# A fused attention and MLP block on one core: load order at the start, denominator, a norm's transposes and two chunks' output sums

## The chip, the cores and the metric

The kernel runs on one core of one Trainium2 chip. The core has five engines that work side by side, each in its own fixed order: TensorE (PE in the profile, with PEld for its weight loads), VectorE (DVE), ScalarE (ACT), GpSimd (POOL) and SyncE (SP). DMA transfers are issued from the queues of SP, ACT and POOL and run beside them. The metric is the device time of one execution in microseconds (us); lower is better.

## The reference

The input `x` has 2048 rows of 512 in bf16. One layer norm, attention in 32 heads of 16 in which each position sees 8 positions (itself and those 2, 4, ... 14 before it), an output projection and a residual; then a second norm, a gated MLP of width 1376 and a second residual.

```python
def _layernorm(x, axis=-1, eps=1e-5):
    m = jnp.mean(x, axis=axis, keepdims=True)
    v = jnp.var(x, axis=axis, keepdims=True)
    return (x - m) / jnp.sqrt(v + eps)
...
        H = 32; Dh = D // H
        W, dil = 8, 2
        qkv = (lambda x, *d: x.transpose(*d))((x @ wqkv).reshape(B, S, 3, H, Dh), 2, 0, 3, 1, 4)
        q, k, v = qkv[0], qkv[1], qkv[2]
        scale = Dh ** -0.5
...
        logits = jnp.einsum("bhsd,bhswd->bhsw", q, kg) * scale
        logits = jnp.where(mask[None, None, :, :], logits, -1e9)
        attn = _softmax(logits, axis=-1)
        o = jnp.einsum("bhsw,bhswd->bhsd", attn, vg)
        return (lambda x, *d: x.transpose(*d))(o, 0, 2, 1, 3).reshape(B, S, D) @ wo
...
        gate = jnp.einsum("bsd,df->bsf", x, W_gate)
        up = jnp.einsum("bsd,df->bsf", x, W_up)
        gate = gate * (lambda x, dt: x.astype(dt))(gate > 0, gate.dtype)
        h = gate * up
        return jnp.einsum("bsf,fd->bsd", h, W_down)
...
    h = x + _A_ref(_layernorm(x, axis=-1), A_wqkv, A_wo)
    h2 = h + _B_ref(_layernorm(h, axis=-1), B_W_gate, B_W_up, B_W_down)
```

## The kernel before

The 2048 rows are four chunks (`tk` 0 to 3) of 512 rows, each of four tiles of 128 rows. `x` stays in SBUF as `x_sm`, and the first residual is added into it in place. All weights are loaded once and stay.

Each chunk goes through these steps. First norm (`layernorm` without `residual`): VectorE takes statistics of each tile (L454, L457), ScalarE makes the reciprocal deviation with Ln and Exp (L467, L471), VectorE normalises (L489), TensorE transposes by four 128x128 matmuls a tile (L518), and ScalarE copies the result out of PSUM (L534; in chunk 0 VectorE does so for tiles 1 and 3, L532). Projections: 12 blocks of four matmuls each (L559), 512 columns wide, which ScalarE copies out (L567) to `qT`, `kT`, `vT`. Logits: VectorE forms products of q with shifted k (L608; in halves in chunk 0, L623), TensorE sums them within each head by a selection matrix (L614), ScalarE takes Exp (L672), which leaves two tiles `ex` of 512 columns, each with four of the eight positions. Denominator: two matmuls into one bank, one for each `ex` (L692), then Ln and Exp on ScalarE (L695, L698). In chunks 1 to 3 VectorE multiplies the `ex` tiles by the reciprocal (L716), and SP broadcasts them over partitions by DMA (L732); in chunk 0 TensorE does the broadcast (L743). VectorE multiplies with shifted v (L764; L779 in chunk 0) and adds up the eight positions: the first of three adds is in chunks 0 to 2 an accumulating DMA of 512 KB issued on POOL (L807), the others run on VectorE (L767, L801 or L771). Output projection: 16 matmuls (L833), residual and row sums (L842 on ScalarE in chunk 0, L844 on VectorE after). Second norm: as the first, with squares on ScalarE (L443); five tile pairs of the second norms are transposed by DMA from SP (`DMAT`, L507) and not by TensorE. MLP: per 128 of the width one block of four matmuls for up and one for gate (L906), copied out by ScalarE (L910 to one of two `up_sb` tiles, L913), multiplied by VectorE (L934); the last 96 of the width go another way (L873 to L892). Down projection: 11 matmuls for each of the four row tiles (L952); VectorE adds the residual from `x_sm` (L963), SP stores 128 KB (L969).

What each engine does in which order is not the source's order. `plan.add` records every step with an engine, a duration, what it waits for and which buffers it takes; `Plan.order` lays the steps out in time by these assumed durations, and of two steps of one engine the one with the lower number in the hand-kept list `RANK` goes first. Buffers come from small pools: 8 PSUM banks, five `row` tiles, two `up_sb` tiles, five `big` tiles. So every engine has one fixed order, and a step that waits holds up everything behind it on its engine. The DMA queues of SP and POOL are such orders too.

At the start `setup` issues the loads. SP takes x tiles 0 and 2, then q and k weight slabs 0 and 2, then chunk 1's x; ACT takes x tiles 1 and 3 and slabs 1 and 3. The v weights and chunks 2 and 3 are held back by small copies on POOL, which write one element of the destination and so make the load wait. TensorE runs 44 matmuls on an empty tile meanwhile (`NWARM`, L408) and 8 each (`NFILL`, L416) after the first transposes of tiles 0 and 1. `GUIDE` holds the second tile's statistics back behind the first's sums, and the third's behind the second's norm. The first four q and k blocks of chunk 0 are cut in three: both column halves for weight slabs 0 and 1, then all columns for slabs 2 and 3.

Of the kernel before, what the change touches and what calls it, by code (L numbers as in the profile page):

```python
# [55 lines left out]
]  # L56


class Op:

# [31 lines left out]
class Plan:  # L92
# [9 lines left out]
    def add(self, key, *a, **k):  # L102
# [8 lines left out]
        return op  # L111


    GUIDE = (("xag0", 0, "xst1", 0), ("xxn1", 0, "xst2", 0))

    def order(self):
        for kx, cx, ky, cy in self.GUIDE:
            xs = [o for o in self.ops if o.key and o.key[0].startswith(kx) and o.key[1] == cx]
            for o in self.ops:
                if o.key and o.key[0].startswith(ky) and o.key[1] == cy:  # L120
                    o.deps = o.deps + xs
# [900 lines left out]
```

## Time and profile before

| what | value |
|---|---|
| time, median of 3 runs | 198.13 us (197.99 to 198.37) |
| span of the profiled execution, first to last instruction | 196.6 us |
| TensorE busy | 190.5 us, 97% of the span |
| VectorE busy | 154.0 us, 78% |
| ScalarE busy | 111.7 us, 57% |
| GpSimd busy | 12.7 us, 6% |

The profiled execution is known by its span alone; what lies around the span is the rest to the measured time. In the windows, each engine has its busy time and, in brackets, its instructions, then the granted TensorE clock as a share, the mean busy share of the 16 DMA engines, and the GB/s they moved. In the timeline, a row is a run of like instructions: start, time to the last one's end, engine, line, operation, output and inputs, count, and in square brackets the idle time before it with what ended it. In the grouped rows come the count, the busy time and the mean of one in ns, then the idle time before the group. Chunks overlap: TensorE does chunk 2's and 3's projections between 36 and 64 us while chunk 0 is still in its attention.

### The profile page before, as it was taken

The page shows a single profiled execution, that of the slowest core. Times are in us where ns is not written, and L with a number is a line of the kernel's source. Part 1 is how long each engine was busy: PE and PEld are TensorE (multiplying, and loading weights), DVE is VectorE, ACT ScalarE, POOL GpSimd, SP SyncE. Part 2 cuts the span into 40 slices and gives each one's busy share as a digit, 9 for nine tenths or more (in the row PEclk, how much of TensorE's full clock was granted, in tenths as well). Part 3 has the DMA queues.
Part 4 walks back from the last instruction along what each step waited for, and adds up shares of the span by engine and source line. Part 5 has one row for each costly group of instructions (what it writes and reads, how often), then busy time and mean ns, then how long its engine had stood idle before and what let it go on. Part 6 is the DMA issues. An engine that isn't in the chain of part 4 may idle for free.

```text
span 196.6 us, 3034 instructions
## 1 busy us (share of the span) xinstructions
PE 190.5 (97%) x1111; PEld 97.1 (49%) x1131; DVE 154.0 (78%) x251; ACT 111.7 (57%) x234; POOL 12.7 (6%) x28
## 2 busy tenths in 40 slices
PE   7899999999999999999999999999999999999994
PEld 7756445654445434464444435444444655444542
DVE  6779999999999999999999779999686331223233
ACT  3548699984598947694334658505674615235400
POOL 4000000330000013100033000000000000000000
PEclk9999999999999999999999999999999999999999
DMA  6969980695000809947369971411002220030114
GB/s 154 310 202 389 405 262 2 122 198 108 3 0 6 196 15 173 188 89 169 81 130 198 181 204 64 82 29 24 3 0 53 53 57 0 0 107 0 27 57 133
DMA packets 21134, 21.99 MB, mean 112 GB/s; under 512 B 8736, under 2 KB 17920, under 8 KB 21120
## 3 DMA queue, kind: packets, MB, share of 16 engines
q1 hardware_dynamic: 18672, 14.65, 25.9%
q0 software_dynamic: 1728, 6.29, 17.2%
q10 hardware_dynamic: 720, 0.85, 1.4%
q8 instruction: 9, 0.15, 0.3%
q14 instruction: 5, 0.04, 0.1%
HBM read 8.42 MB, written 2.10 MB: 53 GB/s over the span
## 4 chain that ended last, share of the span: by engine, by line
PE 66%; DMA 14%; issue 13%; DVE 4%; POOL 1%; SPq 1%; POOLq 0%; DVEq 0%
PE bank L906 20%; PE bank L559 19%; PE bank L952 14%; DMA big<-big 7%; PE bank L833 5%; DMA wv_sb<-in_A_wqkv_dram 4%; PE bank L614 2%; DVE big L764 2%; PE bank L873 2%; PE bank L518 2%; DMA x_sm<-in_A_x_dram 1%; POOL big L807 1%; DMA big<-ex 1%; DVE big L608 1%; PE bank L836 1%
## 5 line engine op out<-in xcount | busy, mean ns | idle before, releaser
L906 PE MATMUL bank<-quad,wgu_sb 128*128 128x512 bf16 x313 | 72.0, 379 | 0.4
L906 PEld LDWEIGHTS <-wgu_sb 128*128 128x128 bf16 x320 | 31.0, 98 | 37.3 <-issue 0.8
L952 PE MATMUL bank<-wd_sb,gT 128*128 128x512 bf16 (+2 forms) x182 | 40.1, 366 | 0.3
L913 ACT ACTIVATE gr<-bank 128x512 bf16<-128x512 f32 x40 | 23.2, 603 | 26.0 <-PE bank L906 24.5
L910 ACT CAST up_sb<-bank 128x512 bf16<-128x512 f32 x40 | 23.2, 594 | 16.5 <-PE bank L906 14.0
L934 DVE TENSOR_TENSOR gT<-gr,up_sb 128x1024 bf16<-128x1024 bf16 x20 | 13.7, 689 | 22.7 <-ACT up_sb L910 16.8
L559 PE MATMUL bank<-quad,wqk_sb 128*128 128x512 bf16 (+1 forms) x132 | 30.2, 367 | 0.2
L952 PEld LDWEIGHTS <-gT 128*128 128x128 bf16 (+1 forms) x187 | 18.1, 98 | 19.5 <-issue 0.4
L764 DVE TENSOR_TENSOR big<-big,vT 128x4096 bf16<-128x4096 bf16 x12 | 27.0, 2283 | 0.1
L608 DVE TENSOR_TENSOR big<-quad,kT 128x4096 bf16<-128x4096 bf16 x12 | 27.0, 2284 | 0.0
L559 PEld LDWEIGHTS <-wqk_sb 128*128 128x128 bf16 x136 | 14.7, 114 | 13.0 <-issue 2.1
L963 DVE TENSOR_TENSOR row<-x_sm,bank 128x512 bf16<-128x512 bf16 (+1 forms) x17 | 10.8, 651 | 9.2 <-PE bank L952 9.2
L767 DVE TENSOR_TENSOR big<-big 128x1024 bf16<-128x1024 bf16 (+2 forms) x24 | 16.8, 729 | 1.2 <-DMA big<-big 1.2
L559 PE MATMUL bank<-quad,wv_sb 128*128 128x512 bf16 x62 | 15.7, 380 | 0.4 <-DMA wv_sb<-in_A_wqkv_dram 0.3
L807 POOL DMA_DIRECT2D big<-big x12 | 10.5, 874 | 85.0 <-DVE big L764 55.0
L833 PE MATMUL bank<-wo_sb,quad 128*128 128x512 bf16 x62 | 14.7, 379 | 0.4 <-DVE quad L801 0.3
L489 DVE TENSOR_SCALAR row<-x_sm,mv,rs 128x512 bf16<-128x512 bf16 x32 | 11.4, 407 | 1.8 <-ACT rs L471 1.8
L534 ACT COPY quad<-bank 128x1024 bf16<-128x1024 bf16 (+1 forms) x11 | 10.0, 944 | 4.5 <-PE bank L518 4.4
L567 ACT CAST kT<-bank 128x512 bf16<-128x512 f32 x16 | 8.9, 598 | 5.7 <-PE bank L559 5.5
L454 DVE BATCH_NORM_STATS2 st<-x_sm 128x6 f32<-128x512 bf16 x16 | 10.3, 675 | 2.1 <-DMA x_sm<-in_A_x_dram 2.1
L567 ACT CAST quad<-bank 128x512 bf16<-128x512 f32 x16 | 9.5, 607 | 3.6 <-PE bank L559 3.6
L443 ACT ACTIVATE row<-x_sm,mv 128x512 bf16<-128x512 bf16 x12 | 8.6, 714 | 4.2 <-DVE mv L435 4.0
(72 smaller groups left out, 157.5 us busy)
## 6 DMA issues: line engine op xcount, KB each, us to landing
big<-big POOLq DMA_DIRECT2D x12, 512.0 KB, 5.4
big<-ex SPq DMA_DIRECT2D x24, 128.0 KB, 2.7
out_dram<-row SPq DMA_DIRECT2D x15, 128.0 KB, 1.8
x_sm<-in_A_x_dram SPq DMA_DIRECT2D x3, 512.0 KB, 4.9
wgu_sb<-in_B_W_up_dram SPq DMA_DIRECT2D x1, 1376.0 KB, 8.8
wgu_sb<-in_B_W_gate_dram SPq DMA_DIRECT2D x1, 1376.0 KB, 11.8
wd_sb<-in_B_W_down_dram SPq DMA_DIRECT2D x1, 1280.0 KB, 15.2
wqk_sb<-in_A_wqkv_dram SPq DMA_DIRECT2D x2, 256.0 KB, 6.9
```

Source lines behind the costliest of these rows:

```text
L559: nc.tensor.matmul(mm.t[:, lo:hi], lhsT=wv_sb[:, dt, t:D:NT] if c == 2 else wqk_sb[:, dt, c * D + t:(c + 1) * D:NT], rhs=xnT.t[:, dt, lo:h ...
L567: nc.scalar.copy(out=o, in_=mm.t[:])
L608: V.tensor_tensor(out=pb.t[:].rearrange("p (t w) s -> p t w s", t=2), in0=q4, in1=k4, op=ALU.mult)
L764: V.tensor_tensor(out=mt.t[:], in0=ab.t[:], in1=v8, op=ALU.mult)
L767: V.tensor_tensor(out=mt.t[:, 0:n, :], in0=mt.t[:, 0:n, :], in1=mt.t[:, n:2 * n, :], op=ALU.add)
L807: nc.gpsimd.dma_start(mt.t[:, 0:4, :], mt.t[:, 4:8, :], accum_op=ALU.add)
L833: nc.tensor.matmul(od.t[:], lhsT=OT.t[:, t, j * P:(j + 1) * P], rhs=wo_sb[:, t, :], start=(t == 0), stop=(t == NT - 1 and tk not in RPE))
L906: nc.tensor.matmul(mm.t[:fs, lo:hi], lhsT=wgu_sb[:, dt, g, ft * P: ft * P + fs], rhs=hnT.t[:, dt, lo:hi], start=(dt == 0), stop=(dt == NT ...
L910: nc.scalar.copy(out=ub.t[:fs, i, :], in_=um.t[:fs, :])
L913: nc.scalar.activation(out=gr.t[:fs, i, :], in_=gm.t[:fs, :], func=ACT.Relu)
L934: V.tensor_tensor(out=gt.t[:fs, 0:n, :], in0=gr.t[:fs, 0:n, :], in1=ub.t[:fs, 0:n, :], op=ALU.mult)
L952: nc.tensor.matmul(od.t[:, c0:c1], lhsT=gts[ft].t[:fs, ft % 2, j * P:(j + 1) * P], rhs=wd_sb[:fs, ft, c0:c1], start=(ft == 0), stop=(ft == ...
```

## The change

It has five parts and a new `RANK` list of 746 entries in place of 737, which sets a new order on every engine.

1. Start. On each of the two queues x tiles and q, k weight slabs alternate: SP x0, slab 0, x2, slab 2; ACT x1, slab 1, x3, slab 3. Chunk 1's x becomes four loads, held back by a POOL copy until x3 has landed; the v weights are held back until weight slab 3 has landed. The gate, up and down weights are loaded in halves (`f_load`), gate first. `GUIDE` goes; the warm-up is 56 matmuls, the fills are 13 and 10; of chunk 0's tiles only tile 1 is copied out by VectorE. Six q and k blocks of chunk 0 are cut, now by column halves: left half for slabs 0 and 1, left half for 2 and 3, right half for all.
2. Denominator of chunks 1 to 3 (`DEN1`): VectorE adds the two `ex` tiles (into one of the five `row` tiles) and TensorE does one matmul.
3. First norm of chunk 3: normalised on ScalarE (`LNA`), transposed by four DMA transposes on SP (two `x` entries in `DMAT`), which in the order stand behind the last weight load and ahead of chunk 1's broadcasts.
4. Output of chunks 0 and 1 (`ODA`): ScalarE copies two row tiles from PSUM into an `up_sb` tile, a DMA on POOL adds these 256 KB into `x_sm`, and SP stores 256 KB from there.
5. The planner's assumed load times.

`LATE` is empty, so what depends on it does nothing.

```diff
-    GUIDE = (("xag0", 0, "xst1", 0), ("xxn1", 0, "xst2", 0))
...
-    DEN1 = ()
+    DEN1 = (1, 2, 3)
...
+    ODA = (0, 1)
+    LATE = ""
...
-    xn_s = o_s = slots(5, [P, D], BF16, "row")
+    es_s = xn_s = o_s = slots(5, [P, D], BF16, "row")
...
+    def f_load(n, i):
+        if n == "d":
+            lo, hi = (0, 5) if i == 0 else (5, NFF)
+            nc.sync.dma_start(
+                wd_sb[:, lo:hi, :], B_W_down[lo * P:hi * P, :].rearrange("(ft p) n -> p ft n", p=P))
+            if FTAIL and i:
+                nc.sync.dma_start(wd_sb[:FTAIL, NFF, :], B_W_down[NFF * P:F, :])
+        else:
+            w = (B_W_gate if n == "g" else B_W_up).rearrange("(dt p) f -> p dt f", p=P)
+            nc.sync.dma_start(wgu_sb[:, 2 * i:2 * i + 2, int(n == "u"), :], w[:, 2 * i:2 * i + 2, :])
...
-        for j in range(BPC):
-            (nc.scalar if j % 2 else nc.sync).dma_start(x_sm[:, j:j + 1, :], x_rows[:, j:j + 1, :])
-        for dt in range(NT):
-            (nc.scalar if dt % 2 else nc.sync).dma_start(wqk_sb[:, dt:dt + 1, :], w3_r[:, dt:dt + 1, 0:2 * D])
-        nc.sync.dma_start(x_sm[:, BPC:2 * BPC, :], x_rows[:, BPC:2 * BPC, :])
+        for i in range(2):
+            for n, q in enumerate((nc.sync, nc.scalar)):
+                j = 2 * i + n
+                q.dma_start(x_sm[:, j:j + 1, :], x_rows[:, j:j + 1, :])
+                q.dma_start(wqk_sb[:, j:j + 1, :], w3_r[:, j:j + 1, 0:2 * D])
...
-        nc.gpsimd.tensor_copy(out=wv_sb[0:1, 0, 0:1], in_=x_sm[0:1, 0, 0:1])
+        nc.gpsimd.tensor_copy(out=x_sm[0:1, BPC:2 * BPC, 0:1], in_=x_sm[0:1, 3, 0:BPC])
+        for j in range(BPC, 2 * BPC):
+            nc.sync.dma_start(x_sm[:, j:j + 1, :], x_rows[:, j:j + 1, :])
+        nc.gpsimd.tensor_copy(out=wv_sb[0:1, 0, 0:1], in_=wqk_sb[0:1, 3, 0:1])
         nc.sync.dma_start(wv_sb[:], w3_r[:, :, 2 * D:3 * D])
...
-    NWARM, NFILL = 44, 8
-    DMAT = (('h',2,0),('h',2,2),('h',3,0),('h',3,2),('h',1,0))
+    NWARM, NFILL = 56, (13, 10, 0)
+    NHALF = 6
...
+    DMAT = (('h',2,0),('h',2,2),('h',3,0),('h',3,2),('h',1,0),('x',3,0),('x',3,2))
...
-    LNA = ((0, 0, 0, 0), (0, 0, 0, 0))
+    LNA = ((0, 0, 0, 1), (0, 0, 0, 0))
...
-                tev = not residual and tk == 0 and j0 % 2
+                tev = not residual and tk == 0 and j0 == 1
...
+            if tk == 0 and n < NHALF:
+
+                a = None
+                for i, (lo, hi, d0, d1, evs) in enumerate(((0, 2 * P, 0, 2, xev[0:2]), (0, 2 * P, 2, NT, []), (2 * P, CS, 0, NT, xev[2:]))):
...
             def f_o(j=j, c0=c0, c1=c1, od=od, ob=ob, tk=tk):
-                if tk in OPE:
+                if tk in ODA:
+                    nc.scalar.copy(out=ob.t[:, j % 2, :], in_=od.t[:])
...
+                def f_oa(j=j, ob=ob, tk=tk):
+                    nc.gpsimd.dma_start(x_sm[:, tk * BPC + j - 1:tk * BPC + j + 1, :], ob.t[:], accum_op=ALU.add)
+
+                def f_o2(j=j, tk=tk):
+                    nc.sync.dma_start(out_rows[:, tk * BPC + j - 1:tk * BPC + j + 1, :], x_sm[:, tk * BPC + j - 1:tk * BPC + j + 1, :])
```

More of the change, by code (lines that the diff above doesn't have):

```diff
@@ L332, in setup @@
         nc.sync.dma_start(wo_sb[:], A_wo.rearrange("(p t) f -> p t f", t=NT))
-        nc.sync.dma_start(wgu_sb[:, :, 1, :], B_W_up.rearrange("(dt p) f -> p dt f", p=P))
-        nc.sync.dma_start(wgu_sb[:, :, 0, :], B_W_gate.rearrange("(dt p) f -> p dt f", p=P))
-        nc.sync.dma_start(
-            wd_sb[:, 0:NFF, :], B_W_down[0:NFF * P, :].rearrange("(ft p) n -> p ft n", p=P))
-        if FTAIL:
-            nc.sync.dma_start(wd_sb[:FTAIL, NFF, :], B_W_down[NFF * P:F, :])
+        for n in "gud":
+            for i in range(2):
+                if n not in LATE:
+                    f_load(n, i)
         for n, (op, by) in enumerate(((ALU.arith_shift_right, 2), (ALU.bitwise_and, H - 1),
@@ L410, with fill @@
     fills = [add(("warm", 0), "PE", 5.7, f_warm, [], -500, take=[wb])]
-    def fill(d):
+    def fill(d, k):
         def f(wb=wb):
-            for _ in range(NFILL):
+            for _ in range(k):
                 nc.tensor.matmul(wb.t[:, 0:P], lhsT=warm[:], rhs=warm[:], start=True, stop=True)
-        fills.append(add(("fill", 0), "PE", 0.056 * NFILL, f, [d, fills[-1]], -400, use=[wb]))
+        fills.append(add(("fill", 0), "PE", 0.056 * k, f, [d, fills[-1]], -400, use=[wb]))
     def layernorm(tk, src, dst_slots, pr, groups, on_act, residual=None):
@@ L567, in f_ev @@
                 nc.scalar.copy(out=o, in_=mm.t[:])
-            wl = wload["qkv"[c]]
-            if tk == 0 and n < 4:
-                ab, done = [wload["ab"]], []
-                for i, (lo, hi, evs) in enumerate(((0, 2 * P, xev[0:2]), (2 * P, CS, xev[2:]))):
-                    done.append(add(("qk%s%d" % ("ac"[i], n), tk), "PE", 2 * MM * (hi - lo) / CS + 0.005,
-                                    lambda f=f_mm, lo=lo, hi=hi: f(lo, hi, 0, 2), evs + ab + done + [fills[-1]], pr - 5,
-                                    take=[mm], use=[xnT]))
-                a = add(("qkd%d" % n, tk), "PE", 2 * MM, lambda f=f_mm: f(0, CS, 2, NT), done + [wl], pr - 4.9, take=[mm],
-                        use=[xnT], lat=PEL)
+            wl = wload["qkv"[c]][0]
+            if tk == 0 and n < NHALF:
+                a = None
+                for i, (lo, hi, d0, d1, evs) in enumerate(((0, 2 * P, 0, 2, xev[0:2]), (0, 2 * P, 2, NT, []), (2 * P, CS, 0, NT, xev[2:]))):
+                    a = add(("qk%s%d" % ("abc"[i], n), tk), "PE", MM * (d1 - d0) * (hi - lo) / CS + 0.005,
+                            lambda f=f_mm, lo=lo, hi=hi, d0=d0, d1=d1: f(lo, hi, d0, d1),
+                            evs + [wload["ab"][0] if i == 0 else wl, a, fills[-1]], pr - 5,
+                            take=[mm], use=[xnT], lat=PEL if i == 2 else 0.0)
             else:
@@ L822, with f_lg @@
                 oev[t] = add(("om%d" % t, tk), "DVE", D2, f_om, [m, rcd], tpr, take=[OT], use=[mt, rc], lat=DL)
+        if tk == 0 and LATE:
+            def f_lg(mt=mt):
+                nc.gpsimd.tensor_copy(out=wgu_sb[0:1, :, 1, 0:1], in_=mt.t[0:1, 0:1, 0:NT].rearrange("p a s -> p s a"))
+                nc.gpsimd.tensor_copy(out=wd_sb[0:1, :, 0:1], in_=mt.t[0:1, 0:1, 0:NFT].rearrange("p a s -> p s a"))
+            lg = add(("lg", tk), "POOL", 0.3, f_lg, [oev[NT - 1]], apr, use=[mt], lat=0.1)
+            for n in LATE:
+                for i in range(2):
+                    wload[n].append(add(("ld" + n, i), "SP", 0.45 + 0.1 * (n == "d" and i), lambda n=n, i=i: f_load(n, i),
+                                        [lg], 0, lat=0.5, dq=(1.0, 1.74)))
         for t in range(NT):
@@ L945 @@
         for n, (j, c0, c1) in enumerate(parts):
-            od, ob = Buf(od_s), Buf(o_s)
+            od = Buf(od_s)
+            if tk not in ODA:
+                ob = Buf(o_s)
+            elif j % 2 == 0:
+                ob = Buf(up_s)
             share = (c1 - c0) / D
@@ L974 @@
                         lambda lo=lo, hi=hi, f=f_dn: f(range(lo, hi)),
-                        [gds[ft] for ft in range(lo, hi)] + [wload["d"], a], mb + 5, take=[od],
+                        [gds[ft] for ft in range(lo, hi)] + wload["d"] + [a], mb + 5, take=[od],
                         use=[gts[ft] for ft in range(lo, hi)], lat=PEL if hi == NFT else 0.0)
+            if tk in ODA:
+                b = add(("o%d" % n, tk), "ACT", A5, f_o, [a], mb - 200, take=[ob], use=[od, ob], lat=AL)
+                if j % 2 == 0:
+                    oa = b
+                    continue
+                def f_oa(j=j, ob=ob, tk=tk):
+                    nc.gpsimd.dma_start(x_sm[:, tk * BPC + j - 1:tk * BPC + j + 1, :], ob.t[:], accum_op=ALU.add)
+                def f_o2(j=j, tk=tk):
+                    nc.sync.dma_start(out_rows[:, tk * BPC + j - 1:tk * BPC + j + 1, :], x_sm[:, tk * BPC + j - 1:tk * BPC + j + 1, :])
+                b = add(("oa%d" % n, tk), "POOL", 1.0, f_oa, [oa, b], mb, use=[ob], lat=1.1, dq=(0.75, 1.5))
+                add(("os%d" % n, tk), "SP", 0.4, f_o2, [b], mb + 6, lat=0.55, dq=(0.3, 0.8))
+                continue
             b = add(("o%d" % n, tk), "ACT" if tk in OPE else "DVE", D5 * share + (0.05 if share < 1 else 0), f_o, [a], mb - 200,
```

30 lines of the change are left out of this document (14 added, 16 removed), and 75 rows, old and new, of the table RANK.

## The prediction

> **What bounds the kernel now.** I read the busy line of the page first, then the windows by stage, then the timeline around every place where TensorE is not busy.
>
> ```profile
> span 196.6 us, 3034 instructions
> PE 190.5 (97%) x1111; PEld 97.1 (49%) x1131; DVE 154.0 (78%) x251; ACT 111.7 (57%) x234; POOL 12.7 (6%) x28
> ```
>
> ```profile
> core 0: us, PE busy (x) PEld busy (x) DVE busy (x) ACT busy (x) POOL busy (x), PEclk, DMA share, GB/s
> 12.20:40.00 27.80, 27.62 (x188) 14.91 (x192) 27.80 (x52) 23.71 (x46) 2.52 (x3) 1.00 0.73 236
> 40.00:64.00 24.00, 23.84 (x155) 11.67 (x157) 24.00 (x31) 17.54 (x43) 1.08 (x2) 1.00 0.32 59
> 64.00:90.00 26.00, 25.84 (x153) 12.16 (x154) 25.88 (x26) 18.02 (x35) 3.45 (x4) 1.00 0.66 137
> 90.00:115.00 25.00, 24.82 (x131) 11.08 (x131) 22.69 (x36) 12.44 (x26) 3.44 (x4) 1.00 0.76 156
> 115.00:140.00 25.00, 24.59 (x122) 11.98 (x126) 24.61 (x38) 12.62 (x28) 0.00 (x0) 1.00 0.26 61
> 140.00:194.00 54.00, 53.45 (x275) 26.57 (x277) 20.60 (x45) 22.04 (x46) 0.00 (x0) 1.00 0.15 41
> ```
>
> ```profile
> 8.76 3.21 PE L559 MATMUL bank<-quad,wqk_sb 128*128 128x256 bf16 x21
> 10.87 1.88 DVE L454 BATCH_NORM_STATS2 st<-x_sm 128x6 f32<-128x512 bf16 x3 [1.92 <-DMA x_sm<-in_A_x_dram]
> 12.22 1.05 PE L559 MATMUL bank<-quad,wv_sb 128*128 128x512 bf16 x4 [0.26 <-DMA wv_sb<-in_A_wqkv_dram]
> 114.04 0.69 DVE L767 TENSOR_TENSOR big<-big 128x1024 bf16<-128x1024 bf16 x1 [1.16 <-DMA big<-big]
> 115.25 3.63 PE L833 MATMUL bank<-wo_sb,quad 128*128 128x512 bf16 x15 [0.33 <-DVE quad L801]
> 193.75 0.42 DVE row L963
> ```
>
> From its first useful matmul at 8.76 to the last copy at 193.75 TensorE is busy in every stage, and it waits in two places: 0.26 us for the v weights and 0.33 us for chunk 2's attention output. So the time is start (8.76) + TensorE work (about 185) + a tail (2.9 us to the span's end). VectorE is a second limiter from 12 to 90: busy 27.80 of 27.80, 24.00 of 24.00, 25.88 of 26. ScalarE and DMA have room. An edit pays if it takes matmuls away or moves 8.76 forward, provided that VectorE gets as much shorter ahead of 90. The span is one execution of 196.6; the median is 198.13, so 1.5 us lie outside the span, and I leave them and the tail (the same last half-block matmuls, copy and store) unchanged.
>
> **The change, part by part.**
>
> *Denominator.* In chunks 1 to 3 one matmul takes the place of two; an add on VectorE precedes it.
>
> ```profile
> L692 PE MATMUL bank<-ex,same 128*128 128x512 bf16 x6 | 1.8, 379 | 0.0
> L716 DVE TENSOR_TENSOR ex<-ex,rec 128x512 bf16<-128x512 bf16 x6 | 2.5, 419 | 0.0
> ```
>
> A pair holds TensorE 1.8/3 = 0.60, one alone 0.38: 3 × 0.22 = **−0.66**. The adds are priced like the same-shaped product, 2.5/6 = 0.42 each on VectorE.
>
> *First norm of chunk 3.* Sixteen transposes leave TensorE for four DMA transposes on SP; two ScalarE copies go; the normalisation goes from VectorE to ScalarE.
>
> ```profile
> 32.25 0.89 PE bank L518 x16
> L489 DVE TENSOR_SCALAR row<-x_sm,mv,rs 128x512 bf16<-128x512 bf16 x32 | 11.4, 407 | 1.8 <-ACT rs L471 1.8
> L443 ACT ACTIVATE row<-x_sm,mv 128x512 bf16<-128x512 bf16 x12 | 8.6, 714 | 4.2 <-DVE mv L435 4.0
> L534 ACT COPY quad<-bank 128x1024 bf16<-128x1024 bf16 x9 | 8.9, 1025 | 4.1 <-PE bank L518 3.9
> ```
>
> TensorE **−0.89**; VectorE −4 × 0.36 (11.4/32) and 0.1 more for one small product; ScalarE +4 × 0.71 − 2 × 1.02 = +0.8.
>
> ```profile
> L507 SPq DMA_TRANSPOSE quad<-row x10: 1188/1216/1269, 95.7 to 152.7; - x10
> DMA to landing us min/median/max: 2.4/2.4/2.5
> L732 SPq EVENT_SEMAPHORE  x18: 17/17/16722, 22.7 to 113.7; - x18
> ```
>
> On SP the four stand behind the last weight loads and ahead of chunk 1's broadcasts: 4 × 1.22 = 4.9 us of issue, hidden in the 16.7 us which SP now stands before its first broadcast. Counting the matmuls in the new order, TensorE wants the result about 25 us after its start, near 34 us. The norms are in place around 28 to 32, the last landing 2.4 later: hardly any slack. I cost it at 0, at most 1.2.
>
> *Start.* Tiles x0, x1 are followed on each queue by a q, k weight slab, and x2, x3 come third. VectorE's order becomes: statistics of x0, x1, norm of x0, statistics of x2, norm of x1, statistics of x3, copy of tile 1, norms of x2, x3. The first useful matmul then hangs on x2's landing.
>
> ```profile
> 3.37 0.69 DVE L454 BATCH_NORM_STATS2 st<-x_sm 128x6 f32<-128x512 bf16 x1 [0.17 <-DMA x_sm<-in_A_x_dram]
> 4.10 0.18 DVE L457 BATCH_NORM_AGGREGATE mv<-st 128x2 f32<-128x6 f32 x1
> 4.20 0.66 DVE L454 BATCH_NORM_STATS2 st<-x_sm 128x6 f32<-128x512 bf16 x1
> 5.67 0.72 DVE L489 TENSOR_SCALAR row<-x_sm,mv,rs 128x512 bf16<-128x512 bf16 x2
> 8.20 0.75 DVE L532 COPY quad<-bank 128x512 bf16<-128x512 bf16 x2
> ```
>
> ```profile
> 1.90:2.90 1.00, 1.00 (x13) 1.00 (x11) 0.93 (x7) 0.27 (x1) 0.55 (x5) 1.00 0.89 242
> 2.90:3.90 1.00, 1.00 (x12) 1.00 (x11) 0.83 (x4) 1.00 (x1) 0.18 (x1) 1.00 0.93 320
> 3.90:4.90 1.00, 1.00 (x12) 1.00 (x10) 0.93 (x4) 0.51 (x3) 0.00 (x0) 1.00 1.03 178
> 4.90:5.90 1.00, 0.97 (x10) 0.70 (x7) 1.00 (x3) 0.51 (x3) 0.00 (x0) 1.00 0.80 158
> 5.90:6.90 1.00, 0.78 (x13) 0.69 (x14) 1.00 (x4) 0.36 (x2) 0.00 (x0) 1.00 0.88 314
> ```
>
> Up to x2 and x3, 1,049 KB have to move (x0, x1 262, two slabs 524, x2, x3 262). At the window rates that is done at 6.4; x0 is used at 3.37, about 0.4 after its 262 KB, so the late bound is 6.8. At 320 throughout from 2.90 it is 5.4 + 0.4 = 5.8. I take the middle, L = 6.3. Then 0.69 (statistics x2) + 0.36 (norm x1) + 0.10 + 0.69 (statistics x3) + 0.10 + 0.38 (copy) + 0.18 (copy to matmul, 8.58 to 8.76) = L + 2.50 = 8.80: **+0.04**, bounds −0.5 and +0.5. Eight of chunk 0's sixteen transposes now come behind that point: 8 × 0.056 = **+0.45**. The v weights are wanted only 8 us into the work, so that wait goes: **−0.26**. The halves' smaller matmuls have the same columns: 0. Chunk 1's x is held back until x3 has landed; that is no later than needed, as VectorE reaches it after the chunk 0 norms: first product about 4.1 after the start, held by ScalarE's copies of q and k, with 0.4 idle in place of 1.92.
>
> The warm-up is 56 matmuls, with fills of 13 and 10.
>
> ```profile
> 0.99 4.88 PE L408 MATMUL bank<-warm 128*128 128x128 bf16 x44 [0.99 <-DVE warm L314]
> 6.12 0.72 PE L518 MATMUL bank<-identity,row 128*128 128x128 bf16 x8 [0.25 <-DVE row L489]
> ```
>
> 44 in 4.88 are 0.11 us each to the end; the transposes at 6.12 run at twice that rate (the sixteen in 0.89 above). The same activity comes first in the new kernel, so I let the twelve more run fast from about 6.1; they end near 6.5, ahead of what x2 allows. If all 56 ran at 0.11, they would end at 0.99 + 6.16 = 7.15, tile 1's transposes near 8.5 and the start would be at 9.2: the sum 0.4 worse. On which of the two it is, the Trainium skill says, in "TensorE: Matmul & The Clock Gate", Part 1 (The HAM clock gate), that the slow phase is about 3.4 us of activity in a free-running window and differs from run to run. This trace, with over 4.6, disagrees on the length; no second execution here shows whether it varies.
>
> *Output of chunks 0 and 1.* Eight VectorE adds go; eight ScalarE copies, four 256 KB accumulating DMAs on POOL and four stores of 256 KB for eight of 128 come.
>
> ```profile
> L963 DVE TENSOR_TENSOR row<-x_sm,bank 128x512 bf16<-128x512 bf16 x15 | 10.1, 682 | 8.6 <-PE bank L952 8.6
> L910 ACT CAST up_sb<-bank 128x512 bf16<-128x512 f32 x40 | 23.2, 594 | 16.5 <-PE bank L906 14.0 <-DVE gT L934 2.5
> 99.13 0.86 POOL L807 DMA_DIRECT2D big<-big  x1 [18.06 <-DVE big L764]
> big<-big POOLq DMA_DIRECT2D x12, 512.0 KB, 5.4
> ```
>
> VectorE −8 × 0.67, ScalarE +8 × 0.59 = 4.7 in stages where it is busy 12 of 25: nothing on TensorE. No row has a 256 KB accumulation; by the 512 KB row it takes 2.7 (half) to 5.4. It blocks twice: its `up_sb` tile is free only after landing, and ScalarE's next copy into it stands in order ahead of all its other copies; and on POOL the first product stands ahead of chunk 2's four. Cover: 6 us of matmuls between the second output block and the next copy into that tile, and 1.9 us more matmuls ahead of chunk 2's output projection than now. I take 0; uncovered it is rival D.
>
> *The weight loads in halves, gate first*: nothing. DMA share is 0.32 after 40, and the first gate and up matmuls come at 64.
>
> *Sum*: −0.66 − 0.89 + 0.04 + 0.45 − 0.26 = −1.32: span 195.3, time **196.8**. VectorE allows it: up to chunk 1's output projection it loses 1.5 of idle time and 1.3 of norm and gains two adds (0.8), −2.0, against TensorE's −1.1 to there.
>
> **The rivals.**
> A, the forecast: own range 196.2 to 197.5, from the start's bounds.
> B: a tight joint takes most of it back: x2 at 6.8 (+0.5), or the slow warm-up, or chunk 3's transposes late (+1.2). For it: the 158 to 178 rows at 3.90 to 5.90 and the missing slack at 34; against: 2.4 is also the longest landing but for 0.1. Time 197.3 to 198.0, say 197.8.
> C: all goes well: start at 8.3 (−0.5), and the 0.33 at 115.25 goes, since four 0.67 adds stood on VectorE between chunk 2's products: −2.15, 196.0.
> D, slower: output products late. Chunk 2's four accumulations now go from 99.13 to the use at 114.04, 3.7 each, the queue full, and the wait at 115.25 is their end. A 256 KB one ahead costs 1.9 + 0.86 issue = 2.8; it decides if over 1.3 of this is uncovered. Fully exposed: 198.13 − 1.32 + 2.8 = 199.6; half, 198.2. The Trainium skill, "DMA: Bandwidth & Descriptors", Anatomy of one DMA, gives 2.0 us + bytes/436 GB/s: an estimate of 2.6 for 256 KB, and 3.2 for the 512 KB that took 5.4 here; by it D would cost 0.6 + 0.86, about 198.3.
> That the change doesn't do what it says I leave out: the built order shows one denominator matmul in three chunks and four DMA transposes.
>
> **How the numbers follow.** A 0.47, C 0.13, B 0.20, D 0.20. Within 0.2% (0.4 us) no measurement of this kernel tells a change. A, C and half of B are faster: 0.70; the rest of B and some of D same: 0.11; slower 0.19. The range from C's 195.7 to most of D, 199.3.
>
> **What would show it.** Right: first q, k matmul at 8.3 to 9.3, no wait on the v weights, transposes of chunk 3 landed by 34, 72 transposes on TensorE for 88, TensorE busy to about 192.4, its share still 97%. Wrong: TensorE idle behind `up_sb` copies at 97 to 105 or ahead of the output projections at 87 and 116, or a matmul near 34 waiting for a DMA transpose.

## The result, and the profile after

The changed kernel takes 197.33 us (median of 22 executions, 196.54 to 198.69) against 198.03 for the kernel before in the same session (22 executions, 197.66 to 198.60). The ratio is 0.9965, 95% interval 0.9952 to 0.9978: 0.70 us faster; the time is 0.5 above the forecast of 196.8 and inside the range. The profiled execution took 197.32 with a span of 195.2.

The busy line and the stages of the changed kernel (start of the window and length, then busy time and instructions of each engine, clock, DMA share, GB/s):

```profile
span 195.2 us, 3072 instructions
PE 189.8 (97%) x1127; PEld 99.3 (51%) x1147; DVE 148.8 (76%) x242; ACT 116.8 (60%) x245; POOL 16.4 (8%) x33
...
12.20:40.00 27.80, 27.37 (x185) 15.18 (x187) 27.64 (x47) 24.61 (x49) 3.15 (x4) 1.00 0.92 268
...
90.00:115.00 25.00, 24.89 (x143) 12.06 (x143) 20.06 (x31) 15.44 (x33) 5.16 (x6) 1.00 0.80 161
115.00:140.00 25.00, 24.84 (x114) 11.31 (x116) 24.18 (x37) 11.89 (x28) 1.72 (x2) 1.00 0.38 77
```

TensorE still fills every stage; its share is 97% as before. VectorE has 20.06 in place of 22.69 from 90 to 115, where chunk 0's adds are gone. The places that the prediction named, in the timeline of the changed kernel (start, length, engine, line, operation, and the idle time ahead of it with what ended it; `SPq` marks what SP issues):

```profile
0.99 5.90 PE L420 MATMUL bank<-warm 128*128 128x128 bf16 x56 [0.99 <-DVE warm L321]
6.20 0.69 DVE L466 BATCH_NORM_STATS2 st<-x_sm 128x6 f32<-128x512 bf16 x1 [0.69 <-DMA x_sm<-in_A_x_dram]
8.10 0.42 DVE L544 COPY quad<-bank 128x512 bf16<-128x512 bf16 x1
8.67 0.60 PE L571 MATMUL bank<-quad,wqk_sb 128*128 128x256 bf16 x4
27.78 5.28 SPq L519 DMA_TRANSPOSE quad<-row  x4
34.59 1.68 PE L571 MATMUL bank<-quad,wqk_sb 128*128 128x512 bf16 x6 [0.22 <-ACT vT L579]
192.12 0.42 DVE L990 TENSOR_TENSOR row<-x_sm,bank 128x256 bf16<-128x256 bf16 x1 [0.19 <-PE bank L977]
```

The start is at 8.67 (8.80 forecast). There is no wait for v weights and none ahead of chunk 2's output projection. TensorE waits 0.22 ahead of chunk 3's first projection at 34.59, where I had seen hardly any slack. The profile puts this wait down to a copy of `vT` by ScalarE, which ended at 34.39; the last of the four DMA transposes had landed just before, at 34.34. The last copy begins at 192.12, 1.63 earlier than in the profile of before. New on the DMA side and in ScalarE's waits:

```profile
x_sm<-up_sb POOLq DMA_DIRECT2D x4, 256.0 KB, 3.5
```

```profile
ACT up_sb L931 <- remote: 3.8, 1, 3.8
```

The accumulating DMA of 256 KB lands in 3.5, between my bounds of 2.7 and 5.4; ScalarE once waits 3.8 for its tile, and TensorE does not notice.

From profile to profile this is −1.4, almost the −1.32 forecast; from median to median it is −0.70. Half of the gain that one profile shows is not in the typical execution, and the experiments ask why.

### The profile page after: what moved, and what is told of

It is laid out like the page before. It is cut to its first block, busy times and chain, and to the rows that moved or that the text cites. A ratio compares the mean times of both kernels' runs of the same rounds, so it can differ in the third digit from the quotient of the medians.

```text
span 195.2 us, 3072 instructions
## 1 busy us (share of the span) xinstructions
PE 189.8 (97%) x1127; PEld 99.3 (51%) x1147; DVE 148.8 (76%) x242; ACT 116.8 (60%) x245; POOL 16.4 (8%) x33
## 4 chain that ended last, share of the span: by engine, by line
PE 85%; DVE 11%; ACT 2%; issue 1%
PE bank L927 35%; PE bank L977 19%; PE bank L571 12%; PE bank L854 7%; DVE big L634 5%; PE bank L625 3%; PE bank L420 3%; PE bank L894 3%; DVE st L466 2%; DVE big L790 2%; PE bank L530 2%; DVE row L501 1%; ACT kT L579 0%; PE bank L857 0%; ACT rs L479 0%
## 5 line engine op out<-in xcount | busy, mean ns | idle before, releaser
L977 PE MATMUL bank<-wd_sb,gT 128*128 128x512 bf16 (+2 forms) x182 | 39.3, 366 | 0.3
L931 ACT CAST up_sb<-bank 128x512 bf16<-128x512 f32 x40 | 22.9, 589 | 19.2 <-PE bank L927 9.5
L571 PEld LDWEIGHTS <-wqk_sb 128*128 128x128 bf16 x152 | 16.4, 114 | 11.6 <-issue 1.9
L501 DVE TENSOR_SCALAR row<-x_sm,mv,rs 128x512 bf16<-128x512 bf16 x28 | 9.8, 406 | 3.3 <-ACT rs L483 3.3
L546 ACT COPY quad<-bank 128x1024 bf16<-128x1024 bf16 (+1 forms) x10 | 8.7, 890 | 4.6 <-PE bank L530 4.6
L571 PEld LDWEIGHTS <-wv_sb 128*128 128x128 bf16 x64 | 6.9, 114 | 6.4 <-issue 0.8
L986 ACT CAST up_sb<-bank 128x512 bf16<-128x512 f32 x8 | 4.5, 586 | 9.5 <-PE bank L977 9.5
```

The costliest lines, as they stand in the source:

```text
L571: nc.tensor.matmul(mm.t[:, lo:hi], lhsT=wv_sb[:, dt, t:D:NT] if c == 2 else wqk_sb[:, dt, c * D + t:(c + 1) * D:NT], rhs=xnT.t[:, dt, lo:h ...
L931: nc.scalar.copy(out=ub.t[:fs, i, :], in_=um.t[:fs, :])
L977: nc.tensor.matmul(od.t[:, c0:c1], lhsT=gts[ft].t[:fs, ft % 2, j * P:(j + 1) * P], rhs=wd_sb[:fs, ft, c0:c1], start=(ft == 0), stop=(ft == ...
```

## The experiments

**The two kernels again.** First both were run unchanged, with a second profile each.

> The kernel before, unchanged, profiled a second time. Theory 1 (the first profiled execution of before was one of its long ones): the span is 195.8 to 196.2 now, not 196.6, with the first useful matmul below 8.7 or less idle time on TensorE than the two waits of 0.26 and 0.33; time minus span is about 2.05, as in the changed kernel. Theory 2 (the profiled execution was typical, and the changed kernel loses something in most of its executions that its profile does not show): span 196.4 to 196.8, time minus span 1.4 to 1.6.

> The changed kernel, unchanged, profiled a second time. Its times went from 196.5 to 198.7, twice the spread of before. Theory 1 (the start varies: landing of x2 and the moment at which TensorE's clock goes up): the span differs from 195.2 by as much as the first useful matmul differs from 8.67, and the stretch from the first useful matmul to the last stays 183.4 within 0.2. Theory 2 (a joint further back is tight: chunk 3's DMA transposes near 34, or the output residual near 97 to 116): the stretch from first to last useful matmul changes by 0.4 or more, with one wait that names the joint.

The kernel before, against itself: 198.41 (197.92 to 199.06, 11 executions), ratio 1.0021 (1.0010 to 1.0032). So two loads of one program can stand 0.2% apart, and variants closer than that are told apart by their profiles, not by medians. Its second profile (span, TensorE's first blocks, last copy):

```profile
span 196.1 us, 3034 instructions
...
8.65 3.21 PE L559 MATMUL bank<-quad,wqk_sb 128*128 128x256 bf16 x21
11.69 1.03 PE L559 MATMUL bank<-quad,wv_sb 128*128 128x512 bf16 x4
...
193.20 0.42 DVE L963 TENSOR_TENSOR row<-x_sm,bank 128x256 bf16<-128x256 bf16 x1 [0.52 <-PE bank L952]
```

The wait for the v weights is gone without any change: 11.69 − 8.65 is 3.04, in the first profile it was 12.22 − 8.76 = 3.46. That is 0.42 of the 0.5 between the two spans. The 29 executions of before beside these runs have a median span of 196.2, so the profile on which I built my sum was longer than most of them. But the 11 executions of this second load have a median of 196.6, and the profiled one is their shortest; how often the wait stands is not shown. Of theory 1 the span and the start came as told; the time outside the span did not, with 1.8 in place of 2.05.

The changed kernel again gave 197.55 (197.01 to 198.26), ratio 0.9977 (0.9965 to 0.9989). Its second profile has a span of 196.1, 0.9 longer than the first:

```profile
7.27 0.69 DVE L466 BATCH_NORM_STATS2 st<-x_sm 128x6 f32<-128x512 bf16 x1 [1.80 <-DMA x_sm<-in_A_x_dram]
...
8.34 0.40 PE L530 MATMUL bank<-identity,row 128*128 128x128 bf16 x4 [1.31 <-DVE row L501]
...
9.62 0.60 PE L571 MATMUL bank<-quad,wqk_sb 128*128 128x256 bf16 x4 [0.33 <-ACT rs L479]
```

VectorE's third statistics wait for their tile until 7.27, 1.07 later than in the first profile, and the start is 9.62, 0.95 later. Everything behind keeps this distance to the end within 0.1: the last copy begins at 193.01, 183.39 after the start, against 183.45. Theory 1 holds here: what differs between the two profiles is the start, and here it follows the landing of one tile by 2.35.

**The denominator alone, undone.**

```diff
-    DEN1 = (1, 2, 3)
+    DEN1 = ()
```

> The changed kernel with two denominator matmuls again in chunks 1 to 3 and no add on VectorE. If TensorE sets the time there, as I forecast: +0.66 (3 x 0.22) over the changed kernel, and TensorE's idle time as before. If VectorE sets it: the three adds of 0.42 come off its order and the time rises by less than 0.3, or falls.

197.83 (197.25 to 198.39), ratio to before 0.9988 (0.9974 to 1.0003). Its profile, first useful matmul and last copy:

```profile
8.96 0.60 PE L571 MATMUL bank<-quad,wqk_sb 128*128 128x256 bf16 x4 [0.33 <-ACT rs L479]
...
193.06 0.42 DVE L990 TENSOR_TENSOR row<-x_sm,bank 128x256 bf16<-128x256 bf16 x1 [0.19 <-PE bank L977]
```

Between the two lie 184.10, in the changed kernel 183.45 and 183.39: the part is worth 0.65 to 0.7. The medians show 0.3 to 0.5, but they hold the starts, too, which vary. The forecast's 0.66 stands.

In this run and in all that add or take away steps, the `RANK` list is written anew, so other work can move in the order, too.

**The first loads in the order of before.**

```diff
-        for i in range(2):
-            for n, q in enumerate((nc.sync, nc.scalar)):
-                j = 2 * i + n
-                q.dma_start(x_sm[:, j:j + 1, :], x_rows[:, j:j + 1, :])
-                q.dma_start(wqk_sb[:, j:j + 1, :], w3_r[:, j:j + 1, 0:2 * D])
+        for j in range(BPC):
+            (nc.scalar if j % 2 else nc.sync).dma_start(x_sm[:, j:j + 1, :], x_rows[:, j:j + 1, :])
+        for dt in range(NT):
+            (nc.scalar if dt % 2 else nc.sync).dma_start(wqk_sb[:, dt:dt + 1, :], w3_r[:, dt:dt + 1, 0:2 * D])
```

> The changed kernel with the first loads in the order of the kernel before (x0 and x2, x1 and x3, then the four q, k slabs); the order of the work is kept. If the changed start hangs on x2's landing: x2 lands about 0.8 to 1.6 earlier (near 5), tile 1's copy ends earlier, and the first useful matmul hangs on the first two slabs instead, which land after 786 KB near 5.5 to 6: start at 7.5 to 8.3, a gain of 0.4 to 1, unless the warm-up ends late (then the start stays within 0.2). If, as the rival has it, x2 does not matter and the slabs do: the start is the same or later, and later blocks wait for the third and fourth slab.

197.21, ratio 0.9960 (0.9947 to 0.9973), and all 5 executions lie between 197.08 and 197.28: in these five the spread is gone, and the median hardly moves. In its profile (lines of VectorE, then TensorE, then SP; numbers of lines are one lower here):

```profile
5.30 0.69 DVE L465 BATCH_NORM_STATS2 st<-x_sm 128x6 f32<-128x512 bf16 x1
...
9.22 0.69 DVE L465 BATCH_NORM_STATS2 st<-x_sm 128x6 f32<-128x512 bf16 x1 [1.02 <-POOL wv_sb L335]
```

```profile
7.64 0.60 PE L570 MATMUL bank<-quad,wqk_sb 128*128 128x256 bf16 x4 [0.29 <-ACT rs L478]
...
25.43 0.40 PE L753 MATMUL bank<-ex,spread 32*128 32x512 bf16 x4 [0.33 <-DVE ex L685]
...
34.66 1.67 PE L570 MATMUL bank<-quad,wqk_sb 128*128 128x512 bf16 x6 [0.51 <-DMA quad<-row]
```

```profile
27.64 5.50 SPq L518 DMA_TRANSPOSE quad<-row  x4
```

The start comes 1.04 earlier, as expected from the landing. All of it is given back by 34.66, 0.07 later than in the changed kernel: TensorE waits for VectorE at 25.43 and for chunk 3's DMA transposes at 34.66. The four stand one behind the other on SP from 27.64 to 33.14, and the last, issued at 31.92, lands at 34.42. VectorE meets chunk 1's x only at 9.22, since that still comes behind the weight slabs, and then runs to 35 without a gap. So a second chain, VectorE to ScalarE to SP, sets the time near 34.6, and it hangs on chunk 1's x: in the three runs with these loads and the full statistics (this one and two further down) the first transpose is issued 18.42 to 18.44 after VectorE takes up that x, at 9.22, 9.55 and 9.74. With the load order of the change the chain comes with the start: there the first transpose is issued 19.11 or 19.12 after the first useful matmul in all seven profiles that have it, for starts from 8.67 to 9.62. So this run does not show that an earlier start would buy nothing in the order of the change.

**Less VectorE work on that chain** (with the loads as in the last run).

```diff
-                        V.bn_stats(out=st.t[:], in_=x_sm[:, tk * BPC + j, :])
+                        V.bn_stats(out=st.t[:], in_=x_sm[:, tk * BPC + j, 0:P] if tk == 3 else x_sm[:, tk * BPC + j, :])
```

> The changed kernel with the first loads in the order of before, as in the run ahead of this one (its start came 1.04 earlier, at 7.64, and all of it was given back by 34.66), and with one thing less: the statistics of chunk 3's x are taken from the first 128 of 512 columns of each row. That takes about 4 x 0.4 = 1.7 us from VectorE between 22.7 and 25.3. Theory V (VectorE, busy without a gap from 9.2 to 35, sets when chunk 3's normalisation and with it the four DMA transposes start): the first transpose is issued near 26 instead of 27.64, the waits of TensorE at 25.43 and 34.66 go, the earlier start is kept: span 194.3 to 194.7, time 196.3 to 196.7. Rival (ScalarE's copies or TensorE's banks hold it there): span 195.2 to 195.4, time within 0.2 of 197.21.

196.90 (196.73 to 196.97), span 195.0: 0.3 gained, not 0.7 to 1.0. This kernel leaves out three quarters of chunk 3's statistics, so it prices the work and is no candidate.

```profile
7.72 0.42 DVE L543 COPY quad<-bank 128x512 bf16<-128x512 bf16 x1 [0.37 <-PE bank L529]
8.29 0.60 PE L570 MATMUL bank<-quad,wqk_sb 128*128 128x256 bf16 x4
...
22.52 0.86 DVE L465 BATCH_NORM_STATS2 st<-x_sm 128x6 f32<-128x128 bf16 x4
...
24.81 0.17 DVE L685 TENSOR_TENSOR ex<-ex,mask 128x16 bf16<-128x16 bf16 x1 [1.29 <-ACT ex L682]
...
27.38 5.39 SPq L518 DMA_TRANSPOSE quad<-row  x4
```

The statistics take 0.86 in place of 2.46, but VectorE then stands 1.29 at the mask of chunk 0, which is ahead in its order and needs a score from TensorE and an Exp from ScalarE. The first transpose is issued at 27.38, only 0.26 earlier. But the start is 8.29 here, 0.65 later than in the run ahead: tile 1's copy waited for its transposes, which came behind the slow warm-up. From the start the first transpose comes 19.09 later, as in the changed kernel, where the run ahead has 20.00. So with less work VectorE no longer holds the chain, as theory V has it, and the wait at 25.43 is gone. The chain then follows the start, through the score and the Exp for which VectorE waits, and TensorE still waits 0.34 for the transposes at 34.34. By this reading the gain in time that theory V told was lost to the late start of this profile; whether in the other four executions, too, is not shown.

**Chunk 3's first transposes on TensorE again.**

```diff
-    DMAT = (('h',2,0),('h',2,2),('h',3,0),('h',3,2),('h',1,0),('x',3,0),('x',3,2))
+    DMAT = (('h',2,0),('h',2,2),('h',3,0),('h',3,2),('h',1,0))
```

> The changed kernel with chunk 3's first transposes on TensorE again (sixteen matmuls and two ScalarE copies of 1.02 for the four DMA transposes; the normalisation stays on ScalarE). By my forecast's term the sixteen matmuls cost 0.89 on TensorE, and 0.16 of wait at 34.6 goes: span +0.7 at the same start, time 198.0 to 198.3. Rival 1 (VectorE sets the pace around 34, and TensorE has time there): +0.3 or less. Rival 2 (the copies on ScalarE are late for the projection): +1.2 or more, with a wait on a quad tile copied by ScalarE near 35.

199.91 (198.66 to 200.19), ratio 1.0080 (1.0057 to 1.0103). Start 9.52, span 198.0: against the second profile of the changed kernel (9.62, 196.1) the part is worth 2.0, of which 1.4 arises at one place:

```profile
34.19 1.11 PE L530 MATMUL bank<-identity,row 128*128 128x128 bf16 x16
35.90 2.37 PE L571 MATMUL bank<-quad,wqk_sb 128*128 128x512 bf16 x9 [0.60 <-ACT quad L546]
```

From 34.19 to 35.90 stand sixteen transposes (0.89) and a wait for ScalarE's copies out of PSUM. That is rival 2. A further 0.3 has come by the last copy, most of it at the denominator matmul at 59.18, which waits for VectorE's add, and 0.3 comes behind the last copy. The matmuls cost what I took for them; undone in this order they also cost a wait that does not stand in the kernel before, where VectorE does the normalisation.

**Half of them on TensorE**, with the loads as before: only `('x',3,0)` stays in `DMAT`.

> The changed kernel with the first loads in the order of before, and only two of chunk 3's four first transposes by DMA; the other two tiles go through TensorE (eight matmuls, 0.45) and one ScalarE copy of 1.02, placed just ahead of chunk 3's first projection. If the four DMA transposes in series on SP (27.64 to 33.14, then 2.4 to landing) hold TensorE at 34.66: SP is done near 30.2, the wait of 0.67 there goes, 0.45 of matmuls is paid: span 194.9 to 195.3, time 196.9 to 197.2. If TensorE's transposes bring a wait for the copy as in the run with all sixteen: span 195.7 to 196.5, time 197.7 to 198.5.

198.39 (197.72 to 198.90), ratio 1.0003 (0.9987 to 1.0019): worse by 1.2 than the load order alone, and by 1.0 in the span of the profile. The wait for the DMA is gone, but the eight transposes and the copy behind them come at the same place:

```profile
33.46 0.61 PE L529 MATMUL bank<-identity,row 128*128 128x128 bf16 x8
34.04 3.02 PE L570 MATMUL bank<-quad,wqk_sb 128*128 128x512 bf16 x11
```

On balance this place costs only 0.2. Some 0.3 of the rest has come by 9.1, where the first matmuls wait for the weight slabs, 0.3 comes at 57.62, where the denominator matmul waits for VectorE's add, and 0.1 behind the last copy. The second of the two forecasts told the span, but little of the loss comes from the cause that it named.

**Chunk 0's output on VectorE again, then chunk 1's.** The same edit with `tk == 0`, then `tk == 1`; the sum is stored from `up_sb`, and the accumulating DMA of that chunk is left away:

```diff
+                if tk == 0:
+                    V.tensor_tensor(out=ob.t[:, j % 2, :], in0=x_sm[:, tk * BPC + j, :], in1=od.t[:], op=ALU.add)
-                if tk in ODA:
+                elif tk in ODA:
                     nc.scalar.copy(out=ob.t[:, j % 2, :], in_=od.t[:])
```

> The changed kernel with chunk 0's output as before on VectorE: four adds of 0.67 into the same up_sb tiles, stored from there, no accumulating DMA for this chunk. Other work around it moves in the order, too. My forecast costed the edit at 0, as it touches nothing on TensorE: then the time stays within 0.3 of the changed kernel. Rival (VectorE is the limit up to 105, where it runs without a gap from 74 to 105, so its adds delay chunk 2's products): +0.7 to +2.0, with TensorE idle ahead of chunk 2's score or output matmuls.

> The changed kernel with chunk 1's output as before on VectorE (four adds of 0.67 into up_sb, stored from there; no accumulating DMA for this chunk). By my forecast's term of 0: within 0.3 of the changed kernel. If VectorE or ScalarE is the limit between 105 and 135: +0.7 to +1.7, TensorE idle behind up_sb or gT tiles there.

Chunk 0: 197.32 (196.59 to 198.68), ratio 0.9965 (0.9947 to 0.9983), the ratio of the changed kernel: nothing. From the start to the last copy its profile has 183.51, as the changed kernel within 0.1. Its median span is 195.5 against 195.3 and its time outside the span 1.79 against 2.05, which nearly cancel. Chunk 1: 199.19 (199.02 to 199.31), ratio 1.0044 (1.0028 to 1.0059). Against the first profile of the changed kernel its span is 1.7 longer; the start is 0.46 later, and 1.1 is lost at one place:

```profile
139.76 2.54 PE L927 MATMUL bank<-quad,wgu_sb 128*128 128x512 bf16 x11
143.33 2.88 PE L854 MATMUL bank<-wo_sb,quad 128*128 128x512 bf16 x12 [1.03 <-DVE quad L812]
```

Between 115 and 140 VectorE is busy 24.18 of 25 in the changed kernel, and four more adds of 0.67 make chunk 3's attention output late. In the kernel before no wait stood at chunk 3's output projection, though VectorE had the adds; there the order was another. The runs price the adds in the new order only.

**The accumulating DMAs twice.**

```diff
                     nc.gpsimd.dma_start(x_sm[:, tk * BPC + j - 1:tk * BPC + j + 1, :], ob.t[:], accum_op=ALU.add)
+                    nc.gpsimd.dma_start(x_sm[:, tk * BPC + j - 1:tk * BPC + j + 1, :], ob.t[:], accum_op=ALU.add)
```

> The changed kernel with each of the four accumulating DMAs issued twice (the last product is added twice in the rows of chunks 0 and 1). If the cover that I named is there: ScalarE's wait for an up_sb tile grows from 3.8 to 5 to 8 us, TensorE's idle time grows by less than 0.3, and the time stays within 0.3. If rival D's joint is near: chunk 2's products on POOL come 0.9 to 2.8 later, TensorE waits ahead of the output projection near 116 or behind up_sb copies near 102, and the time grows by 1 to 2.8.

202.83 (202.53 to 203.19), ratio 1.0242 (1.0228 to 1.0256): +5.3 to +5.5 over the changed kernel's two medians, more than any theory said. ScalarE's waits, the timelines of VectorE and TensorE and the windows around 125:

```profile
ACT up_sb L931 <- DMA x_sm<-up_sb: 12.1, 4, 4.4
```

```profile
113.47 0.69 DVE L778 TENSOR_TENSOR big<-big 128x1024 bf16<-128x1024 bf16 x1 [4.89 <-DMA big<-big]
116.22 1.67 PE L927 MATMUL bank<-quad,wgu_sb 128*128 128x512 bf16 x7 [1.03 <-ACT gr L934]
...
121.51 1.03 PE L927 MATMUL bank<-quad,wgu_sb 128*128 128x512 bf16 x4
124.67 2.96 PE L927 MATMUL bank<-quad,wgu_sb 128*128 128x512 bf16 x8 [2.13 <-ACT up_sb L931]
```

```profile
122.50:125.00 2.50, 0.37 (x3) 0.19 (x2) 0.00 (x0) 0.97 (x2) 0.00 (x0) 1.00 0.10 18
125.00:127.00 2.00, 2.00 (x8) 0.66 (x5) 0.67 (x2) 2.00 (x7) 0.00 (x0) 0.58 0.00 0
127.00:129.00 2.00, 2.00 (x7) 0.76 (x6) 2.00 (x3) 2.00 (x7) 0.00 (x0) 0.57 0.00 0
129.00:131.00 2.00, 2.00 (x11) 0.92 (x10) 1.94 (x6) 1.25 (x4) 0.00 (x0) 1.00 0.01 2
```

The second DMA is issued only when the first has landed, so `up_sb` is held twice as long; ScalarE stands up to 4.4 at the copy, and TensorE waits 2.13 at 124.67. The wait of 1.03 at 116.22 has another root: chunk 2's products stand behind the doubled DMA on POOL, the one that VectorE takes up at 113.47 landed 4.4 later than in the changed kernel (113.44 against 109.00), VectorE stood 4.89 for it, and ScalarE and TensorE wait behind VectorE. So rival D's two joints are both there, at `up_sb` and in POOL's order, and one transfer of 3.5 lies inside their cover, two do not. Behind 124.67 the clock falls to half for 3.4 us, and the matmuls of that stretch come 1.7 later. Whether this made the time longer is not shown: ScalarE was busy 2.00 of 2.00 in both of these windows, and of the four executions the one with a mean clock of 1.000 (the others have 0.989 and 0.990) took 202.81, in the midst of the others (202.53 to 203.19).

**The two best together, and the tiles exchanged.** One run joins the load order of before with chunk 0's output on VectorE:

> The changed kernel with the first loads in the order of before and chunk 0's output on VectorE. Each alone gave 197.2 to 197.3. The chunk 0 part is worth nothing inside the span by its own run, but the time outside the span was 1.79 there against 2.05 to 2.1 in the changed kernel. If that difference belongs to the accumulating DMAs of chunk 0: span 195.2 to 195.4, time 197.0 to 197.1, as steady as with the load order alone (0.2 from lowest to highest). If it is chance: 197.2 to 197.3.

197.28 (196.81 to 197.48), ratio 0.9946 (0.9926 to 0.9966). The span of its profile was 195.6, no better than either. The time outside the span has a median of 1.80 again, so the 1.79 of chunk 0's run was no chance; the span is longer by as much as this gains.

The last run exchanges which queue brings the third tile:

```diff
-                q.dma_start(x_sm[:, j:j + 1, :], x_rows[:, j:j + 1, :])
+                k = j if i == 0 else 5 - j
+                q.dma_start(x_sm[:, k:k + 1, :], x_rows[:, k:k + 1, :])
```

> The changed kernel with the third x tile of each queue exchanged: x3 third on SP's queue and x2 third on ScalarE's. VectorE's third statistics are those of x3, and in the profiles so far the tile on ScalarE's queue landed 0.2 to 1.1 us after the one on SP's in the executions that fell apart most (6.18 and 7.25 against 5.49 and 6.50). If that landing sets the start: third statistics at 5.5 to 6.5, start at landing + 2.35 to 2.5, so 8.1 to 8.9 in place of 8.67 to 9.62, and the spread of the times shrinks; with the joint near 34.6 as floor the span is 194.7 to 195.3, time 196.8 to 197.3. If the queues only change places (the tile issued second is late whichever it is), nothing changes: 197.3 to 197.6 with the same spread.

197.35 (196.93 to 197.94), ratio 0.9949 (0.9929 to 0.9970), span 195.4, start 8.74:

```profile
6.39 0.69 DVE L467 BATCH_NORM_STATS2 st<-x_sm 128x6 f32<-128x512 bf16 x1 [0.86 <-DMA x_sm<-in_A_x_dram]
...
8.74 0.60 PE L572 MATMUL bank<-quad,wqk_sb 128*128 128x256 bf16 x4 [0.32 <-ACT rs L480]
```

Again landing + 2.35. The landing lies among the 5.66 to 7.27 of the other order, so one profile does not show that the queue matters, and the time is that of the changed kernel. No version that does the whole work is faster than the changed kernel by an interval that leaves out the 0.9965 of the changed kernel.

## Why the prediction was right, step by step

**Direction and sum.** From the second profile of before to the first of the changed kernel, the stretch from the first useful matmul to the last copy went from 193.20 − 8.65 = 184.55 to 192.12 − 8.67 = 183.45: −1.10. My terms for this stretch were −0.66 − 0.89 + 0.45 = −1.10. TensorE's busy time in the two stretches (up to the end of the last copy):

```profile
8.65:193.62 184.97, 183.13 (x1035) 90.78 (x1055) 147.32 (x226) 107.94 (x224) 10.64 (x13) 1.00 0.44 107
```

```profile
8.67:192.54 183.87, 182.12 (x1040) 91.86 (x1060) 142.67 (x219) 113.11 (x235) 14.20 (x17) 1.00 0.49 116
```

It fell by 1.01, so the mechanism was right: TensorE sets the time, and less work on it is less time. That the sum meets −1.10 to the last digit is luck. The waits in the stretch fell by 0.09, of which the forecast had nothing: the 0.33 ahead of chunk 2's output projection went, as only rival C had it, and the 0.22 at 34.59 came.

**Denominator, −0.66.** Right: 0.65 by the profile of its undoing.

**Chunk 3's transposes, −0.89.** Right as the price of the matmuls. The landing was costed at 0 with 1.2 as the bound. At 34.34 it was 0.3 later than the "by 34" of the prediction, and it cost at most the 0.22 at 34.59; by the profile this wait is for ScalarE's copy that ended at 34.39. It is the tight joint that I named: with the loads of before the transposes held TensorE there for 0.51, the last of the waits that took back a start 1.04 earlier. That does not exclude rival C's start at 8.3, since with the loads of the change the transposes come forward with the start; no profile of that order has a start before 8.67.

**Start, +0.04.** The form (landing + 2.50) was right where the landing decides: from the third statistics to the first useful matmul it was 2.34 or 2.35 in seven profiles, with starts from 7.64 to 9.62, and 2.47 in the first of the changed kernel. In one more it was 2.43, with a wait for a weight slab, and in three 2.83 to 3.09, for the reason in the next paragraph. My bounds for the landing, 5.8 to 6.8, were too narrow: 5.66 to 7.27. The tile was misnamed: the third statistics are of x3, not x2; with x3 on SP's queue they began at 6.39, 0.02 after SP's tile landed. The starts of this load order spread by a microsecond in the profiles; the times of the changed kernel spread by 2.15 and 1.25 in its two loads. The +0.04 itself came out (8.67 for 8.80) in one profile and not in the other (9.62), so that it did is luck.

**Warm-up.** A second way to be late, which I gave to rival B, was seen where the tile was early, in three profiles. In the run with chunk 0's output on VectorE the tile was there at 5.66, but tile 1's transposes came behind a long slow phase:

```profile
5.66 0.69 DVE L466 BATCH_NORM_STATS2 st<-x_sm 128x6 f32<-128x512 bf16 x1
...
8.18 0.42 DVE L544 COPY quad<-bank 128x512 bf16<-128x512 bf16 x1 [0.63 <-PE bank L530]
```

The warm-up matmuls ran at 0.11 each until 3.7 in the run with the loads as before, until 4.8 and 6.5 in the two profiles of the changed kernel, and at half of that after; the windows' clock column reads 1.00 throughout, so the rate of the matmuls is the better witness at the start. The Trainium skill ("TensorE: Matmul & The Clock Gate", Part 1: The HAM clock gate) says of this phase that it lasts about 3.4 us and varies from run to run. By these runs the second is true; the length was 2.7 to 5.5 from the first matmul at 0.99.

**The v weights, −0.26: wrong in my base.** The wait stands in one profile of before and not in the other. The sum started from a span of 196.6, where the median of 29 executions is 196.2; to credit −0.26 in full was to count as steady a wait that is not.

**Tail and time outside the span, "unchanged": wrong.** From the last copy to the end it is 195.24 − 192.12 = 3.12, in both profiles of before 2.86: +0.26. Of this, 0.1 is the landing of the last store (2.08 after the last copy began, against 1.97), and the rest lies in SP's last waits behind it. Time less span is 2.05 in the median of the changed kernel and 1.78 for before: +0.27. So 196.2 − 1.10 + 0.26 gives 195.4 (median span of the changed kernel 195.3), and with 2.05 it gives 197.4 (measured 197.33). The forecast's span of 195.3 thus met the median by luck: a base 0.4 too long, a wait of 0.26 credited that the second profile does not have and a tail 0.26 too short nearly cancel. The 0.5 that the forecast of the time missed lies outside the span. I had taken 1.5 there, the span of one execution from the median time of others; for before it is 1.78, and for the changed kernel 2.05. Why it grows is open: the medians are 1.9 to 2.1 in eight kernels, the changed one and its variants, but 1.8 in the two with chunk 0's output on VectorE and in the one with the DMAs twice. So the accumulating DMAs alone do not make it, and nothing in a profile shows what does.

**Output of chunks 0 and 1, 0.** Right for chunk 0. For chunk 1 the adds would cost 1.1 ahead of 143.33 in the new order. Cover for the transfer was there, as named. The price was between my bounds; the Trainium skill's formula ("DMA: Bandwidth & Descriptors", Anatomy of one DMA), by which I had estimated 2.6, is too short for these: 3.5.

**The rivals.** B was near: its 197.3 to 198.0 just holds the median, but through the tail and the time outside more than through its joints. Of C the wait of 0.33 went and the early start did not come. D did not come; with the DMAs twice both of its joints showed.

## What to carry to other kernels

Take a second profile of the kernel before you credit a change with removing a wait: a wait of a few tenths that one execution shows may not be in the next. Sum against the median span, and look at the time outside the span as a term of its own. Where the start varies, price a part by the stretch from the first useful matmul to the last copy and not by medians. Where two chains end at the same place, moving one forward buys nothing unless the other comes with it.

## What the runs showed that I had not expected

A wait of 2.13 us on TensorE, 1.03 some 8 us earlier, was followed by half clock for 3.4 us (0.58 and 0.57 over two windows of 2 us). The Trainium skill names an idle window of about 3.4 us as what throttles ("TensorE: Matmul & The Clock Gate", Part 1: The HAM clock gate); here half clock came after 2.13, in the one profile that shows it. And one program, run against itself, stood 0.21% apart (0.10% to 0.32%), with median spans of 196.6 and 196.2.
